# Two transformer layers with sliding-window attention: attention outputs laid out by head in DRAM, and loaded in two parts for the first and the last unit

## The chip, the core and the metric

The kernel runs on one core of a Trainium2 chip. The core has five engines that work side by side, each from a queue of its own that keeps its order: TensorE (PE in the profile; its weight loads are listed as PEld), VectorE (DVE), ScalarE (ACT), GpSimd (POOL) and SyncE (SP). SP computes nothing here; it issues transfers (DMAs). A transfer is moved by the core's 16 DMA engines. The metric is the device time of one execution, in microseconds.

## What is computed

Two layers, each an attention block and then a dense block with squared ReLU, both behind a layer normalisation and with a residual. The two layers share their weights. One sequence of S = 2048 rows, width D = 640, H = 32 heads of 20, a window of W = 256 rows, F = 1536:

```python
def _A_ref(x, wqkv, wo):
    qkv = (x @ wqkv).reshape(B, S, 3, H, Dh).transpose(2, 0, 3, 1, 4)
    q, k, v = qkv[0], qkv[1], qkv[2]
    scores = einsum("bhqd,bhkd->bhqk", q, k) * (Dh ** -0.5)
    mask = (i - j >= 0) & (i - j < W)
    p = softmax(where(mask, scores, -1e9))
    o = einsum("bhqk,bhkd->bhqd", p, v)
    return o.transpose(0, 2, 1, 3).reshape(B, S, D) @ wo

def _B_ref(x, w1, b1, w2, b2):
    r = maximum(x @ w1 + b1, 0)
    return (r * r) @ w2 + b2

for _ in range(2):
    x = x + _A_ref(_layernorm(x), A_wqkv, A_wo)
    x = x + _B_ref(_layernorm(x), B_w1, B_b1, B_w2, B_b2)
```

All is float32 in and out.

## The kernel before

**Units and quads.** The 2048 rows of a layer are cut into eight units of T = 256 rows; over both layers that makes 16 units, numbered u = 0 to 15. Each unit's attention is done in eight quads (NQ = 8) of four heads, which belong to two groups of GQ = 4 quads.

**Dense products** are made in fp16: each float32 operand is split into a rounded half and the rest (high and low), and three of the four products of halves are added up (line 327, the function `mm3`, for all of them, which is why the profile has one line for so much). Units pass through `stage_qk` and `stage_v` (q, k and v from wq_s), `stage_o` (output projection from wo_s), `stage_y` with a layer normalisation, and `stage_f` (w1_s, then w2_s with hh as the squared hidden values). Before the q, k and v products of a unit, its rows are normalised and transposed into yT: `ln_cross(u)` (line 455) for units from 3 on, `ln_t` for the first three.

**A quad of attention** has three steps. `max_quad` ("m") makes score products (lines 652 and 667) and DVE reduces them to row maxima with the mask (line 632). Each group's maxima are turned round by a transposing DMA (line 708) and written as rows into the operand qt (line 688). `exp_quad` ("s") makes the score products again with the maximum taken off (lines 756 and 764), ACT takes the exponentials into pt (line 778), and POOL masks them (lines 793 and 797). `pv_quad` ("v") multiplies by v, with a column of ones that gives the sums (line 827). Score products use two PSUM buffers, bb, so the next "m" can start only when ACT has read those of the "s" before it.

**Outputs.** ACT copies a quad's outputs (pv) into ot (line 839). Every second quad, SP writes both from ot to a DRAM tile o with four DMAs (line 844), one for each head of a quad, of 21 partitions: 20 values and the sum. `load_o` reads a unit's o back so that the products of `stage_o` can use it: the sums, each to four copies (rs, line 870), and the values (val, named od or ov, line 871). It also brings the unit's rows x for the residual (line 885). DVE then takes reciprocals (`ratio`, line 903) and multiplies (`times`, line 906), ACT rounds to the high half of od (line 910), DVE makes the low half (line 913); this goes by quarters of the columns. For most units `load_o(u - 1)` stands behind the first quad of unit u. For the first unit it stands behind its last quad; for the last unit behind everything, ahead of the last projection.

**Order.** The order on PE is worked out when the program is built: `together` interleaves a unit's quads with a stream of dense products, and `flow` does so for the first unit. For the four other engines a planner decides. `post` puts a job with an engine, a cost and a priority into a list that is sorted by priority, and `pump` issues the first job whose operands will be there by its own clock, or a later one that fits before it. `dma` posts to SP; `bulk` posts a weight load, issued by ACT; `need` and `wait_any` move the planner's time on. So a change of one job's cost, priority or operands can move many instructions, PE's too.

**Weights** are loaded once, in the first tens of microseconds, into space that is used for other things later, and split into halves by `convert` (ACT line 259, DVE line 260). `load_wo` loads wo in four pieces by d, and each of the five conversions waits for all four.

**SP's queue** holds, in the planner's order: the rows of maxima (708, 688), the writes of o (844), the loads of `load_o`, x rows, rows of b2 (951) and results (1049).

Of the kernel before, what the change touches and what calls it, by code (L numbers as in the profile page):

```python
# [10 lines left out]
F32 = mybir.dt.float32  # L11
F16 = mybir.dt.float16
# [9 lines left out]
H = 32  # L22
# [23 lines left out]
def kernel(ctx: ExitStack, tc: tile.TileContext, x, wqkv, wo, w1, b1, w2, b2, out):  # L46
# [408 lines left out]
    def ln_cross(u, *deps):  # L455

        ln_load(u, *deps)

        def dst():
            yTs[u] = sb.tile([P, 2, KC, T], F16, name="yT", tag="yT", bufs=1)  # L460
            return yTs[u]

        pre[u] = cross(lns.pop(u), dst, lambda: sb.tile([P, 2, 2, D], F16, name="yl", tag="qd", bufs=1))
# [349 lines left out]
    def pv_quad(n, quad):  # L813
# [18 lines left out]
        if qd == 0:  # L832
            ods[u] = tc.dram_tile([DH + 1, H, T], F32, name=f"o{u}")
        if qd % 2 == 0:
            ots[u] = sb.tile([P, 2, T], F32, name="ot", bufs=2)
        ot = ots[u]

        def out():
            nc.scalar.copy(ot[:, qd % 2], pv)  # L839

        def write():
            drv = ods[u].rearrange("d (q j) n -> j d q n", j=4)
            for j in range(4):
                nc.sync.dma_start(drv[j][:, qd - 1:qd + 1, :], ot[32 * j:32 * j + DH + 1])
# [10 lines left out]

    def load_o(u, late=False, free_=()):

        l, g = divmod(u, NG)
        if late:
            val = sb.tile([P, KC, T], F32, name="ov", tag="qt", bufs=2)  # L860
            od = sb.tile([P, KC, 2, T], F16, name="od", tag="yT", bufs=1)
        else:
            raw = sb.tile([P, 2, KC, T], F32, name="od", tag="hh", bufs=1)
            val = raw[:, 0]
            od = raw[:, 1].rearrange("p c n -> p (c n)").bitcast(F16).rearrange("p (c a n) -> p c a n", a=2, n=T)
        wrote = [ojobs.pop((u, qd)) for qd in range(1, NQ, 2)]
        rs = sb.tile([P, T], F32, name="rs", bufs=1)

        def load():
            nc.sync.dma_start(rs, ods[u][DH:].to_broadcast([4, H, T]))  # L870
# [28 lines left out]
        for i in range(4):  # L899
# [16 lines left out]
            j = post("D", 575, ratio, loaded, prio=pr)  # L916
# [175 lines left out]
    def together(ns, ms, dense, cost, share=1.0, whole=True, after=None, pace=0):  # L1092
# [23 lines left out]
        for k, (part_, what, m) in enumerate(ts):  # L1116
# [39 lines left out]
    def flow(todo, dense):  # L1156
# [3 lines left out]
        while todo:  # L1160
# [21 lines left out]
            else:  # L1182
                pv_quad(n, quad)
            pump()
# [97 lines left out]
```

## Time and profile before

| | |
|---|---|
| runs | 1594.38, 1593.18, 1589.94 us (median 1593.18) |
| the profiled execution | 1590.84 us, its span 1589.1 us |
| mean granted clock of TensorE | 0.997 |
| PE busy | 1558.1 us, 98% of the span |
| PEld | 1167.5 us, 73% |
| DVE, ACT, POOL busy | 983.8, 735.2, 599.5 us (62, 46, 38%) |
| moved by DMA | 160.44 MB, 243209 packets |

The span in 40 slices (one digit is the busy share in tenths, 9 is 90% or more; one slice is 39.7 us; PEclk is the clock that TensorE was granted):

```profile
PE   8989999999999999999999999999999999999999
DVE  8787665656756656665566656557665665756432
ACT  4555535444453444535343453544545345454522
PEclk9999999999999999999999999999999999999999
DMA  9763243362533525343362535434343352441020
```

A time that the chip measures for a whole execution is some 1.7 us more than the span between the first and the last instruction of its profile. Idle time of an engine other than PE costs nothing by itself. In the rows of a group, "3.3 [1.2 <-X]" means that the engine stood idle for 1.2 us just before and that X ended this; the number behind the start is the time to the end of the last instruction of the group.

### The profile page before, as it was taken

The numbers are of one execution on the slowest core, as the hardware profiler recorded it, in microseconds if no ns is written. First come the engines' busy times: TensorE is split into PE (matmuls) and PEld (weight loads), VectorE is DVE, ScalarE is ACT, GpSimd is POOL, SyncE is SP. The second block draws the span as 40 slices with busy tenths as digits, with TensorE's granted clock in tenths as the row PEclk, the third lists the DMA queues.
The fourth block names the chain that finished last, engine by engine and source line by source line (L and its number), as shares of the span: only waits on it lengthen the run. The fifth ranks groups of instructions, "written<-read, shape, count | busy, mean of one in ns | idle before, by whom it ended". The sixth has DMA issues, their size and how long they took to land.

```text
span 1589.1 us, 52465 instructions
## 1 busy us (share of the span) xinstructions
PE 1558.1 (98%) x21534; PEld 1167.5 (73%) x21534; DVE 983.8 (62%) x3253; ACT 735.2 (46%) x1593; POOL 599.5 (38%) x1291
## 2 busy tenths in 40 slices
PE   8989999999999999999999999999999999999999
PEld 7666767777777777778777777777777777776767
DVE  8787665656756656665566656557665665756432
ACT  4555535444453444535343453544545345454522
POOL 1234424334252443525323352442535235353512
PEclk9999999999999999999999999999999999999999
DMA  9763243362533525343362535434343352441020
GB/s 273 206 181 100 70 121 81 100 129 52 121 87 103 110 65 130 69 127 84 97 133 57 122 83 123 92 88 111 69 123 83 98 123 64 111 83 58 29 67 18
DMA packets 243209, 160.44 MB, mean 101 GB/s; under 512 B 91160, under 2 KB 226712, under 8 KB 242968
## 3 DMA queue, kind: packets, MB, share of 16 engines
q1 hardware_dynamic: 236600, 147.58, 38.8%
q10 hardware_dynamic: 6368, 9.50, 2.0%
q8 instruction: 169, 2.77, 0.7%
q14 instruction: 72, 0.59, 0.1%
HBM read 84.68 MB, written 52.95 MB: 87 GB/s over the span
## 4 chain that ended last, share of the span: by engine, by line
PE 91%; DVE 3%; ACT 2%; DMA 2%; SPq 1%; issue 1%; POOL 0%; ACTq 0%; DVEq 0%; POOLq 0%
PE acc L327 70%; PE pv L827 11%; PE bb L652 5%; PE bb L756 5%; DVE bb L632 1%; ACT pt L778 1%; DMA o<-ot 0%; PE bb L764 0%; DMA ov<-o 0%; PE bb L667 0%; SPq L688 0%; DVE qd L509 0%; DVE mx L632 0%; DMA qt<-qk 0%; DMA qk<-qd 0%
## 5 line engine op out<-in xcount | busy, mean ns | idle before, releaser
L778 ACT ACTIVATE pt<-bb 128x512 f32<-128x512 f32 (+1 forms) x736 | 376.9, 603 | 221.8 <-PE bb L756 198.9
L632 DVE CUSTOM_DVE_ANT_0 bb<-bb,maskq 128x320 f32<-128x320 f32 x896 | 409.2, 525 | 95.3 <-PE bb L652 88.6
L793 POOL TENSOR_SCALAR_AFFINE_SELECT pt<-pt 128x256 f32<-128x256 f32 x448 | 188.0, 422 | 558.1 <-ACT pt L778 545.3
L327 PE MATMUL acc<-y,w_s 128*128 128x256 f16 x2880 | 327.9, 273 | 2.1 <-ACT y L377 1.4
L327 PE MATMUL acc<-w_s,hh 128*128 128x320 f16 x2304 | 326.2, 299 | 0.0
L327 PEld LDWEIGHTS <-w_s 128*128 128x128 f16 x2880 | 276.6, 98 | 53.5 <-issue 17.7
L327 PEld LDWEIGHTS <-hh 128*128 128x128 f16 x2304 | 220.5, 98 | 98.4 <-issue 11.5
L327 PEld LDWEIGHTS <-wq_s 128*128 128x128 f16 x2400 | 230.0, 98 | 46.5 <-issue 13.8
L327 PE MATMUL acc<-yT,wq_s 128*128 128x256 f16 x2250 | 259.5, 273 | 2.1 <-DVE qd L509 0.7
L797 POOL TENSOR_SCALAR_AFFINE_SELECT pt<-pt 128x256 f32<-128x256 f32 x512 | 213.5, 438 | 89.2 <-ACT pt L778 87.6
L1012 DVE TENSOR_TENSOR hh<-r,hh 128x256 f16<-128x256 f32 x192 | 94.6, 513 | 213.2 <-ACT hh L1009 206.0
L827 PE MATMUL pv<-pt,vt 128*32 128x128 f32 (+1 forms) x3840 | 191.9, 330 | 0.7 <-POOL pt L797 0.6
L1006 POOL TENSOR_TENSOR r<-r 128x256 f32<-128x256 f32 x192 | 114.3, 615 | 169.5 <-ACT r L1002 167.2
L839 ACT COPY ot<-pv 128x256 f32<-128x256 f32 x128 | 47.8, 373 | 270.0 <-PE pv L827 266.1
L632 DVE DVE_READ_ACCUMULATOR2_ANT mx<- 128x1 f32 x1024 | 145.9, 143 | 0.0
L327 PE MATMUL acc<-wo_s,od 128*128 128x320 f16 x960 | 140.0, 301 | 3.8 <-ACT od L910 3.2
L827 PEld LDWEIGHTS pv<-pt,vt 128*32 128x32 f32 x3840 | 105.4, 109 | 42.1 <-POOL pt L797 6.9
L327 PE MATMUL acc<-wq_s,yT 128*128 128x320 f16 x900 | 131.8, 299 | 1.0 <-DVE y L378 0.5
L327 PEld LDWEIGHTS <-od 128*128 128x128 f16 x960 | 91.7, 98 | 48.7 <-issue 6.9
L1002 ACT ACTIVATE r<-acc,b1s 128x256 f32<-128x256 f32 x192 | 80.9, 473 | 95.9 <-PE acc L327 95.1
L327 PEld LDWEIGHTS <-yT 128*128 128x128 f16 x900 | 85.7, 98 | 39.2 <-issue 6.8
L364 POOL TENSOR_TENSOR bmv<-bmv,neghalf 128x1 f32<-128x1 f32 x64 | 44.2, 696 | 141.3 <-DVE bmv L358 140.8
(95 smaller groups left out, 1225.5 us busy)
## 6 DMA issues: line engine op xcount, KB each, us to landing
qt<-qk SPq DMA_DIRECT2D x30, 480.0 KB
kt<-qk SPq DMA_DIRECT2D x30, 480.0 KB
qk<-qd SPq DMA_DIRECT2D x17, 640.0 KB
o<-ot SPq DMA_DIRECT2D x256, 42.0 KB
od<-o SPq DMA_DIRECT2D x14, 640.0 KB
qk<-yl SPq DMA_DIRECT2D x13, 640.0 KB
qk<-qd SPq DMA_DIRECT2D x17, 320.0 KB
xt<-in_A_x_dram SPq DMA_DIRECT2D x16, 320.0 KB
```

Source lines behind the costliest of these rows:

```text
L327: nc.tensor.matmul(acc, lhs(a, c), rhs(b, c), start=(k == 0), stop=(k == 3 * nk - 1))
L632: nc.vector.tensor_tensor_reduce(out=v, in0=v, in1=mask, scale=1.0, scalar=-3.0e38, op0=ALU.add, op1=ALU.max, accum_out=accum[e, w]),
L652: nc.tensor.matmul(flat[e][rows, o:o + b - a], qt[r, p, i * P + 64 * h:i * P + 64 * (h + 1)], kt[r, p, a + to:b + to], start=True, stop=Tr ...
L756: nc.tensor.matmul(bb[e][rows, k, o + a:o + b], kt[r, 2 * qd + j, ko + 64 * h:ko + 64 * (h + 1)], qt[r, 2 * qd + j, q0 * P + a:q0 * P + b] ...
L778: nc.scalar.activation(box["pt"][:, :o], bb[e][:, k, :o], AF.Exp, scale=SCALE / (QS * QS))
L793: nc.gpsimd.affine_select(out=m, in_=m, pattern=[[0, 2], [-1, P]], compare_op=ALU.is_gt, fill=0.0, base=0, channel_multiplier=1)
L797: nc.gpsimd.affine_select(out=m, in_=m, pattern=[[0, 2], [1, P]], compare_op=ALU.is_ge, fill=0.0, base=0, channel_multiplier=-1)
L827: nc.tensor.matmul(pv[32 * jj:32 * (jj + 1), q0 * P:(q0 + qn) * P], vf[:, c:c + 32], pj[:, j, :], start=(k == 0), stop=(k == len(steps) - ...
L839: nc.scalar.copy(ot[:, qd % 2], pv)
L1002: nc.scalar.activation(box["r"], acc[:, f, :], AF.Relu, bias=b1s[:, f0 + f:f0 + f + 1], scale=1.0 / (YS * WS))
L1006: nc.gpsimd.tensor_tensor(box["r"], box["r"], box["r"], op=ALU.mult)
L1012: nc.vector.tensor_sub(hh[:, 1, f, :], box["r"], hh[:, 0, f, :])
```

## The change

There are six edits.

1. The DRAM tile o of a unit is [6, 32, 4, 256] in place of [21, 32, 256]: value 4c + d of a head lies at [c, head, d], and the sum at [5, head, 0], with three rows of padding behind it that are written but not read.
2. A quad is written when it is done, by four DMAs of 24 partitions (line 841 of the changed kernel). ot has room for one quad and four buffers, where it was two quads and two buffers. There are 512 such issues, of 24 KB each, in place of 256 of 42 KB.
3. Loaded rows of od are ordered (head, d) where they were (d, head), and those of wo_s accordingly: wo is loaded in five pieces by c, each a whole [128, 640] slice, and each conversion waits for its own piece alone.
4. A new function `begin_o` issues the loads of the sums and the values for the quads that are written. For the first and the last unit it is called behind the seventh quad, for seven of the eight quads (112 of 128 partitions); `load_o` then loads the last 16 partitions. For all other units `load_o` calls it once for all.
5. The division (`ratio`) waits for all parts; in the last unit the x rows wait for the last write of o.
6. `ln_cross(3)` posts its jobs with priority 1 in place of 2.

```diff
 def load_wo():
-    v = wo.rearrange("(h c d) n -> d h c n", c=KC, d=4)
+    v = wo.rearrange("(h c d) n -> c h d n", c=KC, d=4)
...
-    loads = []
-    for d in range(4):
-        loads.append(bulk(lambda d=d: nc.scalar.dma_start(raw[d * H:(d + 1) * H], v[d]), H * KC * D * 4, gate0))
     for c in range(KC):
-        woj[c] = convert(raw[:, c], wo_s[:, 0, c], wo_s[:, 1, c], D, loads[-1], *loads[:-1])
+        load = bulk(lambda c=c: nc.scalar.dma_start(raw[:, c], v[c]), P * D * 4, gate0)
+        woj[c] = convert(raw[:, c], wo_s[:, 0, c], wo_s[:, 1, c], D, load)
...
 def ln_cross(u, *deps):
-    ln_load(u, *deps)
+    prio = 1 if u == 3 else 2
+    ln_load(u, *deps, prio=prio)
...
-    pre[u] = cross(lns.pop(u), dst, lambda: sb.tile(...))
+    pre[u] = cross(lns.pop(u), dst, lambda: sb.tile(...), prio)
...
 def pv_quad(n, quad):
...
     if qd == 0:
-        ods[u] = tc.dram_tile([DH + 1, H, T], F32, name=f"o{u}")
-    if qd % 2 == 0:
-        ots[u] = sb.tile([P, 2, T], F32, name="ot", bufs=2)
-    ot = ots[u]
+        ods[u] = tc.dram_tile([KC + 1, H, 4, T], F32, name=f"o{u}")
+    ot = sb.tile([P, T], F32, name="ot", bufs=4)
     def out():
-        nc.scalar.copy(ot[:, qd % 2], pv)
+        nc.scalar.copy(ot, pv)
     def write():
-        drv = ods[u].rearrange("d (q j) n -> j d q n", j=4)
+        drv = ods[u].rearrange("c (q j) d n -> q j c d n", j=4)
         for j in range(4):
-            nc.sync.dma_start(drv[j][:, qd - 1:qd + 1, :], ot[32 * j:32 * j + DH + 1])
+            nc.sync.dma_start(drv[qd, j], ot[32 * j:32 * j + 4 * (KC + 1)])
     jobs.append(post("A", 262, out, prio=0))
-    if qd % 2:
-        ojobs[u, qd] = dma(write, 4 * (DH + 1) * 2 * T * 4, jobs[-1], n=4, cost=350.0)
+    ojobs[u, qd] = dma(write, 16 * (KC + 1) * T * 4, jobs[-1], n=4, cost=350.0)
...
+def begin_o(u, late, upto, *free_):
+    if u not in begun:
...
+        begun[u] = [val, od, sb.tile([P, T], F32, name="rs", bufs=1), 0, []]
+    val, od, rs, at, jobs = begun[u]
+    wrote = [ojobs.pop((u, qd)) for qd in range(at, upto)]
+    begun[u][3] = upto
+    def load():
+        nc.sync.dma_start(rs[16 * at:16 * upto], ods[u][KC, 4 * at:4 * upto, 0:1, :].to_broadcast([4 * (upto - at), 4, T]))
+        nc.sync.dma_start(val[16 * at:16 * upto], ods[u][:KC, 4 * at:4 * upto].rearrange("c h d n -> (h d) c n"))
+    jobs.append(dma(load, 16 * (upto - at) * (KC + 1) * T * 4, *wrote, *free_, n=2, prio=0))
+    return wrote
...
 def load_o(u, late=False, free_=()):
...
-    wrote = [ojobs.pop((u, qd)) for qd in range(1, NQ, 2)]
-    rs = sb.tile([P, T], F32, name="rs", bufs=1)
-    def load():
-        nc.sync.dma_start(rs, ods[u][DH:].to_broadcast([4, H, T]))
-        nc.sync.dma_start(val, ods[u][:DH].rearrange("(c d) h n -> (d h) c n", d=4))
-    loaded = dma(load, P * (KC + 1) * T * 4, *wrote, *free_, n=2, prio=0)
+    wrote = begin_o(u, late, NQ, *free_)
+    val, od, rs, _, parts = begun.pop(u)
+    loaded = parts[-1]
...
-            load_x(i, *([loaded] if u == 0 else ()))
+            load_x(i, *([loaded] if u == 0 else wrote if u == NU - 1 else ()))
...
-        j = post("D", 575, ratio, loaded, prio=pr)
+        j = post("D", 575, ratio, *parts, prio=pr)
...
 # together(), the quads of units 1 to 15, behind a pv_quad
+    if what[1] == NQ * NU - 2:
+        begin_o(NU - 1, True, NQ - 1)
...
 # flow(), the first unit, behind a pv_quad
+    if n == NQ - 2:
+        begin_o(0, False, NQ - 1)
```

What this makes of the instructions' order is shown at three places, on the engines that wait or are waited for there. A row is one instruction (or several alike, "x4") as it stands in an engine's queue, with its line; the changed kernel's lines differ a little from those before.

First, PE in the first quad of unit 2, where the score products of the exponentials (qt and kt_87, line 756, then 755) end and those of the next maximum (line 652) begin. Before:

```order
L756 LDWEIGHTS kt_87
L756 MATMUL bb_134<-qt,kt_87 64x192
L652 LDWEIGHTS qt
L652 MATMUL bb_133<-kt_86,qt 64x256
L652 LDWEIGHTS qt
L652 MATMUL bb_134<-kt_86,qt 64x256
```

After, at the same place:

```order
L755 LDWEIGHTS kt_87
L755 MATMUL bb_134<-qt,kt_87 64x192
L325 LDWEIGHTS wq_s
L325 MATMUL acc<-yT,wq_s 128x256
L325 LDWEIGHTS wq_s
L325 MATMUL acc<-yT,wq_s 128x256
```

Before, the maximum followed at once. Now q products of unit 3 follow, 30 of them, and then the maximum. One quad earlier, behind the exponentials of unit 1's eighth quad, products of the second dense layer stand, 28 before and 12 now, and the last of them run into the maximum:

```order
L325 LDWEIGHTS hh
L325 MATMUL acc<-w_s,hh 128x320
L325 LDWEIGHTS hh
L325 MATMUL acc<-w_s,hh 128x320
L651 LDWEIGHTS qt
L651 MATMUL bb_133<-kt_86,qt 64x256
```

Ahead of the exponentials of unit 1's seventh quad 68 of these products stand now, where 24 stood. In the first unit, PE's order is another too: the eight score products of one exponential step now stand between unit 2's transposes (10 small ones) and unit 2's first q products, and in two quads the "s" and the "m" behind it have only five (with a small transpose) and eight dense products between them.

Second, DVE round the first use of the attention outputs, behind the first reduction (line 632, then 631) of a maximum. rs are the sums, od the outputs; a row with w_s is the second half of a weight conversion. Before:

```order
L632 ISA bb_133,mx<-bb_133,maskq 128x320
L632 ISA mx 128x1
L903 RECIPROCAL rs<-rs 128x64
L906 TENSOR_TENSOR od<-od,rs 128x5x64
L903 RECIPROCAL rs<-rs 128x64 x2
L913 TENSOR_TENSOR od<-od 128x5x64
```

After:

```order
L631 ISA bb_133,mx<-bb_133,maskq 128x320
L631 ISA mx 128x1
L911 RECIPROCAL rs<-rs 128x64
L914 TENSOR_TENSOR od<-od,rs 128x5x64
L911 RECIPROCAL rs<-rs 128x64 x2
L260 SCALAR_TENSOR_TENSOR w_s<-vt_93,w_s 128x640
L921 TENSOR_TENSOR od<-od 128x5x64
```

The reduction stands ahead of the division in both. A conversion of a weight slice has come between the reciprocals and the low half of od. On ACT its first half stands between the copy of the last quad's outputs and the rounding of od:

```order
L836 COPY ot<-pv 128x256
L259 ACTIVATE w_s<-vt_93 128x640
L918 CAST od<-od 128x5x64 x3
```

Before, the rounding followed the copy at once. Third, SP at the end of the program, from the last rows of maxima on. Before:

```order
L688 DMA qt<-mt 1x8x128 x4
L844 DMA o_26024<-ot 21x2x256 x8
L885 DMA x_27223<-xs_127 128x640
L885 DMA x_27223<-xs_128 128x640
L870 DMA rs<-o_26024 128x1x256
L871 DMA ov<-o_26024 128x5x256
```

After:

```order
L687 DMA qt<-mt 1x8x128 x4
L841 DMA o_26327<-ot 6x4x256 x8
L870 DMA rs<-o_26327 112x1x256
L871 DMA ov<-o_26327 112x5x256
L841 DMA o_26327<-ot 6x4x256 x4
L870 DMA rs<-o_26327 16x1x256
L871 DMA ov<-o_26327 16x5x256
L893 DMA x_27548<-xs_127 128x640
L893 DMA x_27548<-xs_128 128x640
```

Seven eighths are loaded ahead of the last write, one eighth behind it, and the x rows have moved behind the loads.

More of the change, by code (lines that the diff above doesn't have):

```diff
@@ L854 @@
     ols = {}
+    begun = {}
+    def begin_o(u, late, upto, *free_):
+        if u not in begun:
+            if late:
+                val = sb.tile([P, KC, T], F32, name="ov", tag="qt", bufs=2)
+                od = sb.tile([P, KC, 2, T], F16, name="od", tag="yT", bufs=1)
+            else:
+                raw = sb.tile([P, 2, KC, T], F32, name="od", tag="hh", bufs=1)
+                val = raw[:, 0]
+                od = raw[:, 1].rearrange("p c n -> p (c n)").bitcast(F16).rearrange("p (c a n) -> p c a n", a=2, n=T)
+            begun[u] = [val, od, sb.tile([P, T], F32, name="rs", bufs=1), 0, []]
[7 more added lines that the diff above has]
+        return wrote
     def load_o(u, late=False, free_=()):
         l, g = divmod(u, NG)
[L859 to L865, printed above, removed]
-        wrote = [ojobs.pop((u, qd)) for qd in range(1, NQ, 2)]
-        rs = sb.tile([P, T], F32, name="rs", bufs=1)
-        def load():
-            nc.sync.dma_start(rs, ods[u][DH:].to_broadcast([4, H, T]))
-            nc.sync.dma_start(val, ods[u][:DH].rearrange("(c d) h n -> (d h) c n", d=4))
-        loaded = dma(load, P * (KC + 1) * T * 4, *wrote, *free_, n=2, prio=0)
+        wrote = begin_o(u, late, NQ, *free_)
+        val, od, rs, _, parts = begun.pop(u)
+        loaded = parts[-1]
         if u == NU - 1:
```

2 lines of the change are left out of this document (1 added, 1 removed).

## The prediction

> **What bounds the kernel now.** I read the busy times by stretches first, then TensorE's waits, then the timeline round each wait. Two of the four stretches of 96.58 us, one unit of 256 rows each, that I looked at (columns: stretch, length, busy time of PE, PEld, DVE, ACT, POOL, granted clock, DMA share, GB/s):
>
> ```profile
> 300.00:396.58 96.58, 96.58 (x1412) 72.81 (x1410) 60.21 (x200) 45.36 (x98) 38.25 (x84) 1.00 0.41 97
> 589.74:686.32 96.58, 96.58 (x1412) 72.81 (x1410) 60.15 (x200) 45.36 (x98) 38.25 (x84) 1.00 0.42 97
> ```
>
> PE is busy for the whole of a unit in the middle, at full clock, and DVE has over a third of its time free. There the new layout can gain nothing; it can only lose, by making PE wait. Something can be gained where PE waits: in the first 210 us and from 1370 us on. The two dearest kinds, in us, times, longest:
>
> ```profile
> PE bb L652 <- ACT pt L778: 8.9, 8, 2.7
> PE acc L327 <- ACT od L910: 3.2, 2, 2.3
> ```
>
> The longest of them, the half clock behind it (window rows), and a shorter one late in the program, behind which the clock stays:
>
> ```profile
> 201.47 0.75 PE L756 MATMUL bb<-qt,kt 62*64 62x192 f16 x32
> 202.31 3.05 ACT L778 ACTIVATE pt<-bb 128x512 f32<-128x512 f32 x6 [3.13 <-PE bb L756]
> 204.93 0.27 PE L652 MATMUL bb<-kt,qt 60*64 60x256 f16 x1 [2.70 <-ACT pt L778]
> 205.42 0.75 PE L652 MATMUL bb<-kt,qt 60*64 60x256 f16 x37 [0.23 <-ACT pt L778]
> 203.34:206.75 3.41, 1.60 (x54) 1.14 (x57) 0.43 (x2) 2.03 (x5) 2.66 (x8) 1.00 0.73 224
> 206.76:210.16 3.40, 3.40 (x34) 2.03 (x27) 3.36 (x16) 0.37 (x1) 0.00 (x0) 0.50 0.94 293
> ...
> 1376.75 0.75 PE L756 MATMUL bb<-qt,kt 62*64 62x192 f16 x32
> 1377.44 1.67 PE L327 MATMUL acc<-wo_s,od 128*128 128x320 f16 x11
> 1380.21 0.27 PE L652 MATMUL bb<-kt,qt 60*64 60x256 f16 x1 [1.10 <-ACT pt L778]
> 1376.70:1380.10 3.40, 2.41 (x44) 1.63 (x44) 1.55 (x5) 2.50 (x6) 1.67 (x5) 1.00 1.14 216
> ```
>
> In both places the score products of the next maximum (L652) start 3.46 us after those of the exponentials (L756): ScalarE must first empty the banks. Dense products standing between fill that time; at 202 us none stand there. A half clock follows a window with 1.60 us of work in 3.41, none follows one with 2.41 in 3.40.
>
> **Unit 3's normalisation.** Ranked higher, it lets the q products of unit 3 be ready when unit 2's first quad has started its exponentials: 30 of them stand there now. The attention's place moves with it: 68 products of the second dense layer run ahead of unit 1's seventh quad, and only 12 behind its eighth. At 1.67 us for 11, 12 take 1.8; with 0.7 for L756, 0.95 of the 3.46 us stay idle where 2.70 were: 1.75 won. The clock: 3.4 us at 0.50 cost half of it, 1.7, and 0.95 idle is less than the 1.10 behind which it stayed at 1380 us. I take -3.4. Bounds: 0, if the 68 products only postpone the wait; -4.6 (2.70 + 0.23 + 1.7), if nothing of it is left.
>
> The Trainium skill, page "TensorE: Matmul & The Clock Gate", part 1, says that the array falls to half rate after at least one idle window of some 3.4 us. By that rule these waits cost no clock, and the term would be -1.75. Here the trace differs: clock 0.50 stands behind waits of 2.70 and 0.23 us.
>
> **Seven of eight quads ahead, at the end.** The last unit's outputs are written, read back, divided by their sums and split before the output projection (the line with 6.25 is of the chain of waits, the last of the page's DMA issues):
>
> ```profile
> 1517.21 1.34 SPq L844 DMA_DIRECT2D o<-ot  x4
> 1519.92 0.59 SPq L870 DMA_DIRECT2D rs<-o  x1
> 1520.56 6.25 DMA ov<-o
> 1525.84 0.96 DVE L903 RECIPROCAL rs<-rs 128x64 f32<-128x64 f32 x2 [1.92 <-DMA rs<-o]
> 1529.16 0.45 PE L327 MATMUL acc<-wo_s,od 128*128 128x320 f16 x2 [0.88 <-ACT od L910]
> 1529.87 1.40 PE L327 MATMUL acc<-wo_s,od 128*128 128x320 f16 x9 [0.27 <-DVE od L913]
> ...
> ov<-o SPq DMA_DIRECT2D x2, 640.0 KB
> ```
>
> 640 KB take 6.25 us, and PE waits 0.88 + 0.27. Now seven eighths go out behind the seventh quad, on SP ahead of the eighth's write, whose data is not there before 1517.2 anyway. The last eighth, 80 KB, need only land 1.2 us sooner than 6.25 for both waits to go; at half of 6.25, taken as an upper estimate for an eighth of the bytes, it is 3 us sooner: -1.15. PE's order there is the same as before. The x rows that now follow the loads on SP are first needed behind the projection's products. Bounds: 0 and -1.15.
>
> **The start.** PE's order is another here, and three things count. First, the wait for unit 2's transposed input:
>
> ```profile
> 69.64 0.70 PE L327 MATMUL acc<-wq_s,kt 128*128 128x320 f16 x4 [1.00 <-DVE yT L378]
> 66.80:70.20 3.40, 1.98 (x11) 1.07 (x11) 3.14 (x13) 1.23 (x3) 0.00 (x0) 1.00 0.73 234
> 70.23:73.63 3.40, 3.40 (x20) 1.94 (x20) 1.71 (x4) 1.64 (x4) 1.53 (x4) 0.50 1.01 310
> 77.90 0.50 PE L764 MATMUL bb<-qt,kt 62*128 62x256 f16 x8
> 78.34 1.67 PE L327 MATMUL acc<-wq_s,kt 128*128 128x320 f16 x11
> 79.94 0.73 PE L667 MATMUL bb<-kt,qt 60*128 60x128 f16 x8
> ```
>
> A quad's 8 exponential products (0.5 to 0.8 us) now stand between the transposes and that wait: -0.8. The window then holds some 2.6 us of work, more than the 2.41 that kept the clock: -1.7. Second, two quads get shorter cover: L667 came 2.04 us after L764 with 11 products between and no wait; five products and a small transpose (0.8) behind 0.5 leave some 0.6 open, eight (1.1) some 0.4: together +1.0.
>
> Third, the first use of the outputs (with a conversion of a weight slice on ACT and on DVE, L259 and L260):
>
> ```profile
> 112.85 0.75 PE L652 MATMUL bb<-kt,qt 60*64 60x256 f16 x37 [0.23 <-ACT pt L778]
> 113.74 0.50 DVE L632 CUSTOM_DVE_ANT_0 bb<-bb,maskq 128x320 f32<-128x320 f32 x1 [0.73 <-issue]
> 114.16 0.55 DVE L903 RECIPROCAL rs<-rs 128x64 f32<-128x64 f32 x1
> 115.48 0.37 ACT L839 COPY ot<-pv 128x256 f32<-128x256 f32 x1 [2.69 <-PE pv L827]
> 117.69 0.45 PE L327 MATMUL acc<-wo_s,od 128*128 128x320 f16 x2 [2.29 <-ACT od L910]
> 118.02:121.42 3.40, 3.13 (x13) 1.74 (x13) 3.40 (x13) 0.48 (x2) 0.00 (x0) 0.50 1.22 205
> 103.59 0.73 ACT L259 ACTIVATE w_s<-kt 128x640 f16<-128x640 f32 x1
> 109.21 0.82 DVE L260 SCALAR_TENSOR_TENSOR w_s<-vt,w_s 128x640 f16<-128x640 f32 x1
> ```
>
> PE waits 2.29 us here, and loading ahead does not remove it. The division is queued on DVE behind the first reduction (L632) of a maximum that PE starts at 112.85, and it stands there still. What is new is a weight slice between: ACT converts it (0.73) after the copy of pv and before the first cast of od, DVE (0.82) behind that and before it splits od. Both lie on the chain from 112.85 to 117.69, partly beside each other: +1.0, nearer to the longer one with what waits on both than to their sum. Its bounds: -4.3 (2.29 + 0.27 at 118.4 us and the clock's 1.7) and +1.6. The start together: -0.8 - 1.7 + 1.0 + 1.0 = -0.5.
>
> **More writes, and the wo loads.** 256 issues of o become 512, and SP's four take 1.34 us. In the middle they are hidden in SP's spare time, at a price of nothing; what it costs without that cover is the first rival. wo comes in five loads of whole slices in place of four that all had to land; its conversions start earlier on ACT and DVE, which is in the new orders that I counted above.
>
> **Sum.** -3.4 - 1.15 - 0.5 = -5.05. The profiled execution took 1590.84 us (span 1589.1 and 1.7 round it), so 1585.8. It lies 2.3 below the median of the three runs, 1593.18, from which the same sum gives 1588.1. I forecast **1586.5**, nearer to the run whose rows I used; its own range is 1582 to 1588.4.
>
> **Rivals.** (1) Slower: SP becomes the brake. Behind a write of o that waits for ScalarE's copy stand the transposed maxima (L708) and the rows of qt (L688), and the next exponentials' products wait for these:
>
> ```profile
> 633.07 3.64 SPq L688 DMA_DIRECT2D qt<-mt  x4
> 641.33 0.75 PE L756 MATMUL bb<-qt,kt 62*64 62x192 f16 x32
> ...
> 1369.91 3.62 SPq L688 DMA_DIRECT2D qt<-mt  x4
> ```
>
> From the rows' last issue (636.71) to their use pass 4.62 us; 3.22 were enough at 1373.53 to 1376.75. That leaves 1.40 us in the tightest group of a unit. One more write (1.34) just fits. It decides from the second on: 2 x 1.34 - 1.40 = 1.3 us per unit, 13 units, +17: 1590.8 - 4.55 + 17 = 1603. For it: SP keeps order, and each transpose now has a write ahead. Against it: a write's data is copied well before the maxima behind it are reduced. Chance 0.13. The skill's page "DMA: Bandwidth & Descriptors", Rules for kernel authors, warns against transfers under 64 KB as mostly overhead; these shrink from 42 to 24 KB, and no row here shows PE paying for it.
>
> (2) The change does less than it says: the clock drops remain or come elsewhere, as by the skill's rule they have nothing to do with such waits. Then -5.05 + 3.4 = -1.7: 1589.1 from the profiled run, 1591.5 from the median. For it: the window of 66.8 us had 1.98 us of work and still lost its clock, so the threshold is not sharp. Chance 0.19.
>
> (3) The start's wait goes as well: -4.3 in place of +1.0, sum -10.4, 1580.5. For it: seven eighths are loaded early. Against it: the reduction ahead of the division. Chance 0.10.
>
> **Numbers.** The forecast's case has 0.58. A measurement of this kernel tells 0.3% (4.8 us) from no change, that is below 1588.4. Faster: 0.58 + 0.10 = 0.68; within: 0.19; slower: 0.13. Range: from 1580, the third rival, to 1594, the second with the median's offset and some loss in the middle; left out are the first rival and the far ends.
>
> **What would show it.** Right, if PE's wait for pt near 200 us is about 1 us and no clock of 0.50 follows; if no wait for od stands before the last projection; if one for od, with clock 0.50 behind it, still stands before the first, some 3 us long; if a middle unit still takes 96.58 us with PE busy throughout. Wrong, if PE waits for L688's rows in the middle, if the half clock near 70 us stays, or if a new wait follows the 68 products.

## The result and the profile after

| | before | after |
|---|---|---|
| median of the runs | 1591.95 us (6 runs, 1589.94 to 1594.38) | 1601.71 us (6 runs, 1596.09 to 1605.65) |
| profiled execution, span | 1590.84, 1589.1 us | 1605.03, 1603.3 us |
| PE busy | 1558.1 us | 1567.1 us |
| mean granted clock | 0.997 | 0.994 |

The change made the kernel slower: the ratio is 1.0057, with a 95% interval of 1.004 to 1.0074, and the medians lie 9.8 us apart. 1586.5 was forecast, and 1594 was the end of the range. The profiled execution is one of the longest of its six, so sizes below come from medians and places from the trace.

PE's waits after the change (us in total, times, longest):

```profile
PE bb L651 <- ACT pt L777: 7.7, 8, 2.6
PE acc L325 <- ACT od L918: 3.3, 1, 3.3
PE pv L826 <- POOL pt L796: 2.8, 7, 0.9
PE bb L666 <- ACT pt L777: 2.7, 1, 2.7
```

The first two rows look as before. New are a wait of `pv` for POOL's masks and one of 2.7 us of a maximum (L666) in the first unit. The middle of the program shows most. This is the stretch from the first `pv` product of unit 3 to that of unit 14, where PE's order is the same in both, before and then after (length, busy time of PE, PEld, DVE, ACT, POOL, clock, DMA share, GB/s):

```profile
309.76:1362.26 1052.50, 1052.47 (x14950) 792.26 (x14946) 653.11 (x2177) 488.44 (x1062) 409.73 (x892) 1.00 0.42 98
```

```profile
317.63:1374.44 1056.81, 1055.04 (x14949) 792.69 (x14945) 652.53 (x2177) 485.34 (x1062) 411.30 (x892) 1.00 0.42 98
```

The same work takes 4.3 us more. 1.7 of them are idle time, and by 2.6 the products' busy time is longer, at full clock. PE comes to unit 3 later by 7.9 us (317.63 less 309.76), though that stretch holds the place where 3.4 were to be won.

Three places went as forecast. Unit 2's first quad, where the wait was 2.70 us with a half clock behind it, and the window behind the wait:

```profile
205.79 1.80 PE L325 MATMUL acc<-w_s,hh 128*128 128x320 f16 x12
208.55 0.27 PE L651 MATMUL bb<-kt,qt 60*64 60x256 f16 x1 [0.96 <-ACT pt L777]
```

```profile
208.01:211.42 3.41, 2.64 (x73) 1.75 (x73) 1.58 (x8) 1.08 (x4) 1.78 (x5) 1.00 0.27 103
```

The last projection follows the products ahead of it with no wait for od. (The last unit is still no shorter in this execution, 142.56 us behind 1460.74 where it was 140.91 behind 1448.19: two half clocks of 3.41 us fall into it, at up to 1.7 us each, and none before.)

```profile
1530.82 11.58 PE L325 MATMUL acc<-w_s,hh 128*128 128x320 f16 x84
1542.32 8.58 PE L325 MATMUL acc<-wo_s,od 128*128 128x320 f16 x60
```

And a wait for od of 3.3 us still stands before the first projection, as the list of waits shows.

**The middle.** Each write of o takes SP longer. The durations of SP's issues (least, median, most in ns), before and after:

```profile
L844 SPq DMA_DIRECT2D o<-ot x256: 267/311/1677, 58.3 to 1518.2; - x128
```

```profile
L841 SPq DMA_DIRECT2D o<-ot x512: 670/687/1806, 49.1 to 1533.6; - x171
```

There are twice as many, and each takes 0.69 us in place of 0.31, though it carries 24 KB and no longer 42. Four of them now hold SP for 2.9 us, eight times a unit. What this does is seen in unit 5 (timeline; after, SP, then POOL, ACT and PE, here and below one engine behind another; ... stands for rows of the same engine that are left out):

```profile
550.49 2.95 SPq L841 DMA_DIRECT2D o<-ot  x4
...
554.81 1.52 SPq L959 DMA_DIRECT2D xt<-in_B_b_dram  x1
562.98 3.31 POOL L966 TENSOR_TENSOR x<-x,xt 128x320 f32<-128x320 f32 x4 [1.79 <-DMA xt<-in_B_b_dram]
...
568.50 0.41 POOL L792 TENSOR_SCALAR_AFFINE_SELECT pt<-pt 128x256 f32<-128x256 f32 x1 [1.07 <-ACT pt L777]
566.90 0.41 ACT L1017 CAST hh<-r 128x256 f16<-128x256 f32 x1 [2.90 <-POOL r L1014]
...
567.78 0.59 ACT L777 ACTIVATE pt<-bb 128x512 f32<-128x512 f32 x1
573.76 1.18 PE L826 MATMUL pv<-pt,vt 128*32 128x256 f32 x8 [0.28 <-POOL pt L796]
```

The same place before:

```profile
540.81 1.38 SPq L844 DMA_DIRECT2D o<-ot  x4
...
543.19 1.45 SPq L951 DMA_DIRECT2D xt<-in_B_b_dram  x1
551.89 3.31 POOL L958 TENSOR_TENSOR x<-x,xt 128x320 f32<-128x320 f32 x4
555.81 0.41 ACT L1009 CAST hh<-r 128x256 f16<-128x256 f32 x1 [1.08 <-POOL r L1006]
...
557.35 0.60 ACT L778 ACTIVATE pt<-bb 128x512 f32<-128x512 f32 x1 [0.56 <-PE bb L756]
```

Unit 5 starts 9.27 us later after the change (its first `pv` product at 512.19 for 502.92). Take that off, and the b2 rows (line 959) are issued 2.35 us later than before and POOL's addition of them starts 1.82 us later. POOL squares the hidden values behind it; ACT, which keeps order, stands at the rounding of these squares (2.90 us) and starts the exponentials 1.16 us late; POOL's masks are late, and PE's `pv` products wait for them. Four engines hand on a delay that began at SP.

### The profile page after: what moved, and what is told of

It reads as the page before. It is cut to its first block, busy times and chain, and to the rows that moved or that the text cites. A ratio compares the mean times of both kernels' runs of the same rounds, so it can differ in the third digit from the quotient of the medians.

```text
span 1603.3 us, 52930 instructions
## 1 busy us (share of the span) xinstructions
PE 1567.1 (98%) x21534; PEld 1170.5 (73%) x21534; DVE 983.7 (61%) x3253; ACT 731.2 (46%) x1593; POOL 600.1 (37%) x1291
## 4 chain that ended last, share of the span: by engine, by line
PE 82%; DMA 4%; DVE 4%; ACT 4%; POOL 3%; SPq 2%; issue 1%; ACTq 0%; POOLq 0%; DVEq 0%
PE acc L325 62%; PE pv L826 10%; PE bb L755 4%; PE bb L651 4%; ACT pt L777 2%; DMA xt<-in_B_b_dram 2%; DVE bb L631 2%; SPq L841 1%; POOL r L1014 1%; POOL x L966 1%; DMA qk<-qd 1%; ACT r L1010 1%; POOL pt L796 1%; SPq L687 1%; DMA o<-ot 0%
## 5 line engine op out<-in xcount | busy, mean ns | idle before, releaser
L826 PE MATMUL pv<-pt,vt 128*32 128x128 f32 (+1 forms) x3840 | 195.8, 332 | 3.4 <-POOL pt L796 2.8
```

Source lines behind the costliest of these rows:

```text
L826: nc.tensor.matmul(pv[32 * jj:32 * (jj + 1), q0 * P:(q0 + qn) * P], vf[:, c:c + 32], pj[:, j, :], start=(k == 0), stop=(k == len(steps) - ...
```

## The experiments

All ran against the kernel before, whose median in these comparisons was 1591.9 to 1592.3 us. The 95% interval of a ratio to it reaches 1.4 to 2.4 us either way (2.7 for the changed kernel), so a step of 2 us from one run to another is not certain by the medians alone. The line numbers of a run are its own.

**1. The writes' shape: plain blocks (run four_plain).**

```diff
-        ods[u] = tc.dram_tile([KC + 1, H, 4, T], F32, name=f"o{u}")
+        ods[u] = tc.dram_tile([H, P // 4, T], F32, name=f"o{u}")
...
-            nc.sync.dma_start(drv[qd, j], ot[32 * j:32 * j + 4 * (KC + 1)])
+            nc.sync.dma_start(ods[u][4 * qd + j, :4 * (KC + 1)], ot[32 * j:32 * j + 4 * (KC + 1)])
...
-    v = wo.rearrange("(h c d) n -> c h d n", c=KC, d=4)
+    v = wo.rearrange("(h d c) n -> c h d n", c=KC, d=4)
```

The loads follow this order of rows; it holds for all later runs but b2_by_act and those made from the kernel before.

> The changed kernel, but a head's 24 rows lie together in DRAM, so that each of the 512 writes is one plain block of 24 rows of 256 and no longer 6 x 4 x 256; same number of writes, same bytes, same order on TensorE. Theory A (the shape makes an issue on SP 0.69 us long, and the b2 rows behind the writes come late): an issue takes about 0.3 us, POOL no longer waits for the b2 rows, a middle unit takes 96.58 us again, and the 6.5 us that were lost between unit 2 and unit 14 are gone: about 1595. Theory B (it is the number of writes, whatever their shape): waits and time as in the changed kernel, about 1602.

1595.75 us, ratio 1.0024 (1.0015 to 1.0033): 6.0 under the changed kernel. SP's issues and the middle stretch:

```profile
L840 SPq DMA_DIRECT2D o<-ot x512: 289/363/2217, 51.4 to 1524.9; - x171
```

```profile
316.01:1368.48 1052.47, 1052.45 (x14949) 792.21 (x14945) 653.00 (x2177) 487.63 (x1062) 409.49 (x892) 1.00 0.44 99
```

With as many writes of as many bytes, an issue takes 0.36 us, and the middle is as long as before the change. Theory A holds: it is the form of the transfer that makes SP slow. The 6.5 us that the expectation names were its 4.3 and some 2 in unit 2.

**2. One write for each quad (run one_write).**

```diff
-            for j in range(4):
-                nc.sync.dma_start(...)
+            nc.sync.dma_start(ods[u][4 * qd:4 * qd + 4].rearrange("h d n -> (h d) n"), ot)
```

> As the run before, but with one write of 128 rows of 256 for each quad (32 rows a head, 8 of them never read): 128 issues in place of 512, 128 KB each. Theory A: SP is as free as before the change or freer, a middle unit takes 96.58 us, about 1595. Theory B: the same 1595, since the number is small, so that it parts from A only in the run before. Theory C (the new order of work on the engines is what costs in the middle, not SP): waits as in the changed kernel, about 1602. If the bytes moved count (a third more per write), it is slower than the run before.

1594.14 us, ratio 1.0014 (1.0005 to 1.0023). A quarter of the issues brings 1.6 us more, which the two intervals do not tell from nothing. The Trainium skill, page "DMA: Bandwidth & Descriptors", Rules for kernel authors, advises to join transfers under 64 KB. In these runs joining four times 24 KB into 128 KB brought 1.6 us, and the form of the 24 KB is worth 6.0.

**3. The b2 rows off SP's queue (run b2_by_act).** The changed kernel with its dear writes, and one edit:

```diff
-        load = dma(lambda: nc.sync.dma_start(b2s, ...), P * D * 4)
+        load = dma(lambda: nc.scalar.dma_start(b2s, ...), P * D * 4)
```

> The changed kernel with its dear writes; only the b2 rows are issued from ScalarE's queue and no longer from SP's, behind the writes. Theory A1 (the b2 rows' lateness is the link from SP to PE): POOL waits for xt vanish from the middle, the drift between unit 3 and unit 13 (3.7 us in the profile of the changed kernel, 4.3 from unit 3 to unit 13) goes, about 1596 to 1597, a little less gained than with plain writes, since an issue takes ScalarE's time. Rival A2 (it is the rows of maxima or the loads of o behind the writes): waits stay, about 1602.

1595.31 us, ratio 1.0017 (1.0005 to 1.0028): 6.4 under the changed kernel, a little more than expected. POOL's waits for the b2 rows (us, times, longest), before and after the change and in this run, and this run's middle:

```profile
POOL x L958 <- DMA xt<-in_B_b_dram: 9.3, 2, 7.6
```

```profile
POOL x L966 <- DMA xt<-in_B_b_dram: 26.4, 13, 7.7
```

```profile
POOL x L966 <- DMA xt<-in_B_b_dram: 8.0, 1, 8.0
```

```profile
312.13:1365.07 1052.94, 1052.70 (x14949) 792.42 (x14946) 651.00 (x2177) 487.54 (x1062) 412.10 (x892) 1.00 0.42 98
```

SP still spends 0.69 us on each of 512 issues, and the loss is gone. So the link from SP to PE in the middle is this one load, not the rows of the maxima. (PE waited for these rows for 1.1 us in all after the change, 0.90 of them in unit 2; with plain writes, in four_plain, 0.62 us stand there.)

**4. Unit 3's ranking alone (run prio_only).** The kernel before, with `prio = 1 if u == 3 else 2` in `ln_cross`.

> The kernel before with one edit: unit 3's normalisation at priority 1. The prediction's term: the wait of 2.70 us near 202 us becomes about 0.95, and the half clock behind it goes: -3.4, about 1588.5. Rival 1 (the clock's drop has nothing to do with the wait): -1.75, about 1590. Rival 2 (the wait only moves): 1592.

1589.09 us, ratio 0.9983 (0.9974 to 0.9992): -3.1, where -3.4 was forecast. The wait is 0.42 us here, with 16 products in front and no half clock behind. The profiled executions bear it out in place: from a wait of 0.52 us in unit 1 (141.61 us before, 142.11 here) to one of 1.10 us in unit 14 (1380.21 and 1377.15) this run takes 3.56 us less. That is more than the 2.28 us that the wait itself lost.

**5. The slice loads in the kernel before (run wo_slices).**

```diff
-        v = wo.rearrange("(h c d) n -> d h c n", c=KC, d=4)
+        v = wo.rearrange("(h c d) n -> c d h n", c=KC, d=4)
...
+            load = bulk(lambda c=c: nc.scalar.dma_start(raw[:, c], v[c]), P * D * 4, gate0)
+            woj[c] = convert(raw[:, c], wo_s[:, 0, c], wo_s[:, 1, c], D, load)
```

> The kernel before with one edit: wo in five loads by slice, each conversion waiting for its own. This alone gives the start of TensorE's order in the changed kernel (to unit 1's second quad). Theory S (the start is lost by this order: short cover, a weight slice in the chain of the first od): some 8 us lost by unit 1's fifth quad, as in the profile of the changed kernel, about 1600, with a wait of 2.7 us for pt near 60 us and one of about 3 us for od near 120 us. Rival (the start is lost by the dear writes on SP): within 1 us of before, about 1592.

1602.25 us, ratio 1.0065 (1.005 to 1.008). The size is near the 1600 expected, but its place is not:

```profile
50.26 0.37 PE L762 MATMUL bb<-qt,kt 62*128 62x256 f16 x1 [5.39 <-DVE bmv L356]
```

This wait of 5.39 us and one of 3.24 (at 53.87, for the rows of maxima) stand at the very start, before any od; the changed kernel has none of this size there. DVE, on which the first depends, stood for 5.52 us until rows of x had landed. Rows of o in the kernel before are ordered (d, head), so a slice had to be a [4 x 32 x 640] load here and was [32 x 4 x 640] in the change. This run therefore says nothing of the change's start. The Trainium skill, page "DMA: Bandwidth & Descriptors", section "Why a DMA increments its semaphore by 16 and not by 1", says that a load runs on the largest number of engines, up to 16, that divides the slowest dimension of both its sides, which here would be 4. That would fit, and no run separates it.

**6. wo in four loads again (run wo_four).** The one-write run with

```diff
-            woj[c] = convert(..., load)
+            woj[c] = convert(..., loads[-1], *loads[:-1])
```

and four loads of 32 partitions.

> The run with one write for each quad, but with wo loaded in four pieces again, each conversion waiting for all four, as in the kernel before. Theory S (the start is lost by the new way of loading wo): the one-write run lost 6 us against before until unit 2's first quad, apart from unit 3's ranking; without it 1588 to 1589, below the kernel before by 3 to 4 and at or below the run with the ranking alone. Rival (the start's loss comes from writing quad by quad): about 1594, as the one-write run. The order near the first od has no dense products between the exponentials and the next maximum, so a wait of about 3 us may stand there in place of the one for od.

1593.31 us, ratio 1.0001 (0.9987 to 1.0014): the expectation was missed by some 5 us, and the rival's 1594 is nearer. The profiled execution took 1588.12, but the twelve runs lie between 1587.93 and 1599.05. The wait for od is gone, and waits of 2.43, 2.01 and 2.38 us round it took its place.

**7. Slices and quads, one at a time (runs slices_alone, quads_alone).** Both with plain writes, the ranking, and no early load. slices_alone keeps the slice loads and writes after every second quad; quads_alone writes after each and loads wo in four pieces.

```diff
 # slices_alone
-        ojobs[u, qd] = dma(write, 16 * (KC + 1) * T * 4, jobs[-1], n=4, cost=350.0)
+        if qd % 2:
+            ojobs[u, qd] = dma(write, 4 * (DH + 1) * 2 * T * 4, jobs[-1], n=4, cost=350.0)
 # quads_alone
-            woj[c] = convert(..., load)
+            woj[c] = convert(..., loads[-1], *loads[:-1])
```

> Of the changed kernel the slice loads of wo and unit 3's ranking, with plain writes after every second quad and no early load; rows by head, so that a slice is one [32 x 4 x 640] load as in the changed kernel and not [4 x 32 x 640] as in the run with slices before. With writes by quad too it is the no-early-load run (1593.1), without both it is the run with the ranking alone (1589.1). Theory S (the slices' order costs): about 1593. Theory Q (writing quad by quad makes the worse order): about 1589.

> The other half: one plain write after each quad and unit 3's ranking, wo in four loads, no early load. Theory S: about 1589. Theory Q: about 1593. If both are near 1591, the loss is shared.

1592.26 us (1.0002; 0.9993 to 1.001) and 1595.60 us (1.0022; 1.0011 to 1.0033). With the next run they make a square: neither 1589.1, slices 1592.3, quads 1595.6, both 1593.05. Each costs against the ranking alone, and together they don't cost the sum. Theory S and theory Q are both too simple: each edit changes the planner's order of the first 200 us into another one with its own waits.

**8. The early loads (runs no_early_load, early_at_end).** The one-write run with both calls of `begin_o` ahead of time left out, and with the first unit's left out.

```diff
 # both runs
-                if n == NQ - 2:
-                    begin_o(0, False, NQ - 1)
 # no_early_load alone
-                if what[1] == NQ * NU - 2:
-                    begin_o(NU - 1, True, NQ - 1)
```

> The one-write run without the early load: both the first and the last unit load all eight quads at once; TensorE's order is the same. The prediction's term for the end: waits of 0.9 + 0.3 us for od before the last projection come back, +1.15, and at the start nothing changes, because the reduction and the weight slice stand ahead of the division: about 1595.3. Rival (the early load shortens the start's chain too): the wait for od near 119 us grows beyond 3.9 us, 1596 or more.

> The one-write run (1594.1, early load for the first and the last unit) with the early load for the last unit alone; TensorE's order is the same. Theory E (the end's term pays about 1.5, the first unit's early load costs 2 to 3, because the planner then puts a weight slice and a maximum's reduction ahead of the division): the wait for od near 117 us is 2.3 + 0.3 us as in the no-early-load run and not 3.9, no wait for od stands before the last projection, about 1591.5. Rival (the early load does nothing measurable at either end): 1593 to 1594.

1593.05 us (1.0003; 0.9994 to 1.0012) and 1591.45 us (0.9996; 0.9985 to 1.0006), against 1594.14 with both. For the first, 1595.3 was expected: the first unit's early load does count, and against the kernel. The second came out at 1591.5 as theory E says, with 2.29 us of wait before the first projection. At the end the early load takes out waits of 1.48 + 0.28 us, and the median falls by 1.6. In the first unit it costs 2.7. The profiled executions bear out both in place. Up to the wait of 0.52 us in unit 1, one_write takes 147.22 us and early_at_end 143.60. And from the wait of 1.86 us for pt in the last unit to that of 1.40 us before its dense block, executions with no half clock between take 89.05 us (before) and 89.09 (prio_only) without the early load, 87.51 (four_plain) and 87.71 (one_write) with it. Round the first projection, with both early loads (one_write):

```profile
118.77 0.37 ACT L836 COPY ot<-pv 128x256 f32<-128x256 f32 x1 [3.70 <-PE pv L826]
119.03 0.74 ACT L259 ACTIVATE w_s<-vt 128x640 f16<-128x640 f32 x1
119.70 0.46 ACT L916 CAST od<-od 128x320 f16<-128x320 f32 x1
122.56 3.84 PE L325 MATMUL acc<-wo_s,od 128*128 128x320 f16 x13 [3.90 <-ACT od L916]
```

without them (no_early_load):

```profile
114.30 0.66 DVE L912 TENSOR_TENSOR od<-od,rs 128x320 f32<-128x320 f32 x1
117.30 0.37 ACT L836 COPY ot<-pv 128x256 f32<-128x256 f32 x1 [3.61 <-PE pv L826]
117.57 0.46 ACT L916 CAST od<-od 128x320 f16<-128x320 f32 x1
119.51 0.45 PE L325 MATMUL acc<-wo_s,od 128*128 128x320 f16 x2 [2.30 <-ACT od L916]
```

With the early load the planner puts a weight slice (L259) between the copy and the rounding, and on DVE a reduction ahead of the division; without it there is neither. In no_early_load the rounding starts 2.6 us after the first quarter of od is divided (114.96), and the copy of `pv`, ahead of it on ACT, waits for PE in this time. In one_write the division itself ends only at 119.66 (it runs for 0.49 us from 119.17, behind 1.65 us for which the profile names no releaser), so there the copy is not all that holds the rounding up.

**9. The rounding ahead of the copy (run cast_first).**

```diff
-        jobs.append(post("A", 262, out, prio=0))
+        jobs.append(post("A", 262, out, prio=2 if n == NQ else 0))
```

> The no-early-load run (1593.1) with one instruction moved: on ScalarE the first rounding of od stands ahead of the copy of pv of unit 1's first quad and no longer behind it; every other engine's order is the same. Theory P (the prediction's: the division, behind the reduction on DVE, holds the first od up): no change of the wait of 2.3 us before the first projection, 1593. Theory K (ScalarE's copy, which waits for pv, holds it up, since the division is done 2.6 us before the rounding in the no-early-load run): the wait falls to about 1 us, since the second rounding still stands behind the copy; 1591 to 1592, less if a half clock goes with it.

1594.35 us, ratio 1.0013 (1.0004 to 1.0022), where theory K expected 1591 to 1592, so nothing was won. But:

```profile
115.89 0.46 ACT L916 CAST od<-od 128x320 f16<-128x320 f32 x1 [2.12 <-DVE od L912]
117.50 0.37 ACT L836 COPY ot<-pv 128x256 f32<-128x256 f32 x1 [1.15 <-PE pv L826]
118.28 4.50 PE L325 MATMUL acc<-wo_s,od 128*128 128x320 f16 x30 [0.89 <-ACT od L916]
126.19 2.54 PE L325 MATMUL acc<-wo_s,od 128*128 128x320 f16 x12 [3.40 <-DVE x L944]
```

The wait for od falls from 2.30 to 0.89 as theory K says, and 3.40 us appear a few products later: DVE stands for 3.01 us until the residual's rows x have landed, the projection's results can't be taken off, and PE waits for DVE. In this execution the next load in SP's queue set the end of that stretch. Such a wait, of 2.29 us, stands in four_plain's execution too, which has not this edit; so the run shows what held od up, and not what the edit is worth.

**10. What paid, together (run end_only).** Ranking, plain writes after every second quad (singly for the last two quads of the last unit), four loads of wo, early load at the end.

```diff
 # against the kernel before
+        prio = 1 if u == 3 else 2
...
+            for q in qs:
+                nc.sync.dma_start(ods[u][4 * q:4 * q + 4].rearrange("h d n -> (h d) n"), ot[:, q % 2])
...
+                if what[1] == NQ * NU - 2:
+                    begin_o(NU - 1, True, NQ - 1)
```

> What is left when only the parts that paid are kept: unit 3's ranking, plain writes of 128 rows (two after every second quad, as the planner had it before), wo in four loads, the early load for the last unit alone. TensorE's order is exactly that of the run with the ranking alone (1589.1). Theory (the end's term of the prediction holds): its waits of 0.98 + 0.27 us for od before the last projection go, about 1588, 4 us under the kernel before. Rival (as in the first unit, an early load costs more than it brings): 1589 or more.

1589.91 us, ratio 0.9991 (0.9982 to 1.0). 1588 was expected, and the median falls on the rival's side (1589 or more); it doesn't part from the ranking alone (0.9974 to 0.9992). No od wait stands before its last projection, so the 1.2 us are gone there, but the total doesn't show them. Both versions are well below the changed kernel; the ranking alone is the one that is clear of no change.

## Why the prediction was wrong

Medians, each run one part away from the next:

| part | from, to (us) | measured | forecast |
|---|---|---|---|
| unit 3's ranking | 1592.2, 1589.1 | -3.1 | -3.4 |
| slices and writes by quad: a new order, above all at the start | 1589.1, 1593.05 | +4.0 | -0.5 for both rows of the start |
| early load at the end | 1593.05, 1591.45 | -1.6 | -1.15 |
| the start: early load for the first unit | 1591.45, 1594.14 | +2.7 | (in the -0.5) |
| four writes for a quad, not one | 1594.14, 1595.75 | +1.6 | 0 |
| each of them 6 x 4 x 256 | 1595.75, 1601.71 | +6.0 | 0 |

The rows add up to +9.5, and -5.05 was forecast. Of the 14.5 us between them the two rows of the writes make some 7.6, and the new order and the first early load, where the start was to win 0.5, some 7. A row under 2 us is not certain by itself; for the end the traces bear it out (1.4 in place, run 8), for four writes against one they don't. The +4.0 need not all lie in the start: the profiled executions of the two runs part by 1.0 us up to the wait of 0.52 us in unit 1. Later, a longer wait for od at the end (1.48 for 0.98 us) and a half clock more stand in the second.

**Unit 3: right**, in place and size. 0.95 us of wait were forecast and 0.96 stand there; the 68 products left no wait behind. The clock stays at 1.00. By the rule that the prediction cites from the Trainium skill, page "TensorE: Matmul & The Clock Gate", part 1, the term would have been -1.75. The interval of the run with the ranking alone, -1.3 to -4.1 us, holds both; the half clock that went from this place and the 3.56 us that its trace won round it speak for -3.4.

**The end: right.** Both waits went, PE's order was the same, and the stretch is 1.4 us shorter where no half clock falls into it. That this pays in the total is seen in one pair of medians (-1.6) and not in the other (end_only against the ranking alone, +0.8).

**More writes: the step that failed.** "SP's four take 1.34 us" was carried over from a 21 x 2 x 256 write to one of 6 x 4 x 256. The new one takes 2.9. With 1.34 the sentence "in the middle they are hidden" would have held: with plain writes (1.45 for four) the middle is 1052.47 us long. The trace before had a warning in SP's own list: its rows of maxima, 1 x 8 x 128, take 0.63 us an issue with only 2 KB.

**The first rival** had the engine and the mechanism, and not the place: its slack of 1.40 us was that of the rows of maxima, whereas the b2 rows broke first, and its 17 us for 13 units were some 6. It let one more write of 1.34 us just fit; what broke the fit was the length of an issue.

**The start: wrong, sign and all.** Waits were taken from the trace before and moved to a new order one by one. Taken one by one in the changed kernel's trace, they came out as follows.

The 0.8 us ahead of unit 2's first products were not won. Waits of 0.56, 0.24 and 1.00 us stood round its transposes before; 0.61, 0.73 and 0.52 us stand there now.

The half clock near 70 us came earlier in this execution, from 64.64 us on, behind a wait that the forecast had put at nothing. There 20 products stand between the exponentials and the next maximum, as before. But ACT, which keeps order, stood at a rounding of q (line 505) until a transfer out of the same buffer had landed, with three of the four exponentials behind it:

```profile
61.92 0.60 ACT L505 ACTIVATE qd<-acc 128x512 f16<-128x512 f32 x1 [2.91 <-DMA qk<-qd]
63.34 0.76 PE L666 MATMUL bb<-kt,qt 60*128 60x128 f16 x8 [2.72 <-ACT pt L777]
```

Seven more runs have this order of PE there (1, 2, 3, slices_alone, both of 8, and 9). In their profiled executions this wait is 1.0 to 1.4 us, and only four_plain has a half clock between 60 and 76 us. So the term for the clock held in six of eight executions, and the wait in its place was left out.

The short cover of two quads (together +1.0) cost less. The maximum waited for ACT behind neither; ahead of the five products PE waited 0.77 us for DVE's low half of q, where 0.6 had been put. (By the prediction's own figures, 2.04 - 0.8 - 0.5, it would have been 0.74.)

The wait for od grew by 1.0 (3.32 against 2.29), as forecast, and the two conversions that were named stand in it. Wrong was the premise that the division, behind the reduction, holds the first od up:

```profile
119.00 0.49 DVE L914 TENSOR_TENSOR od<-od,rs 128x320 f32<-128x320 f32 x1
120.08 0.37 ACT L836 COPY ot<-pv 128x256 f32<-128x256 f32 x1 [3.57 <-PE pv L826]
120.35 0.74 ACT L259 ACTIVATE w_s<-vt 128x640 f16<-128x640 f32 x1
120.98 0.45 ACT L918 CAST od<-od 128x320 f16<-128x320 f32 x1
121.12 0.82 DVE L260 SCALAR_TENSOR_TENSOR w_s<-vt,w_s 128x640 f16<-128x640 f32 x1 [0.75 <-ACT w_s L259]
```

The first quarter was divided at 119.49 us, and ACT's copy of `pv` came only at 120.08. Before, too, the rounding followed the copy (115.48 and 0.37 us). Run 9 shows the same for an order with no reduction ahead.

One half clock was counted behind this wait, as before. The trace has three: from 115.85 to 119.26 and from 122.68 to 129.50 us. Two more cost up to 3.4 us; the other runs with this order of PE have two to four.

So the step that failed at the start is to carry waits over singly, with ACT's other work and further half clocks at nothing. Why slices and quads cost 3.2 and 6.5 alone and 4.0 together stays open: the orders differ at many places, and each has its own waits.

The third rival did not come: the first od wait did not go. Of the second a part did. The clock behind unit 3's wait held, but half clocks came elsewhere: the profiled execution has six windows of them, the one before three.

## What to carry to other kernels

Before counting a changed transfer at an old price, find a row with its own shape: here the same 24 KB cost SP 0.36 or 0.69 us an issue, and that alone made 6 us. When a queue becomes slower, look for the load in it with the least slack, over all that share the queue and not only over the ones that PE names, and follow it through the engines that keep order. A gain that is sized in one place (unit 3) could be kept without the rest of the change; the start, whose order comes from a planner, was not priced rightly by moving its waits one by one.

## What the runs showed of the hardware

- The length of an issue on SP went by form and not by size here (medians): 128 x 256 in one block 0.34 us, 24 x 256 in one block 0.36, 21 x 2 x 256 0.31, 6 x 4 x 256 0.69. In the last the 24 partitions are cut in two dimensions; that this is the cause was not tried.
- The same pair of waits costs a half clock in one execution and none in another. Before, waits of 1.86 and 0.58 us begin at 1454.40; after, 1.85 and 0.58 at 1466.95. Before, the pair falls into two windows, with 1.77 us of PE's work in the first and 2.61 in the second, and the clock stays at 1.00. The first:

```profile
1452.63:1456.04 3.41, 1.77 (x40) 1.16 (x33) 3.33 (x8) 2.74 (x6) 1.56 (x4) 1.00 0.05 10
```

After, it falls into one, with a half clock behind it:

```profile
1467.50:1470.92 3.42, 1.55 (x54) 1.09 (x57) 3.42 (x9) 2.86 (x7) 3.08 (x6) 1.00 0.02 2
1470.93:1474.34 3.41, 3.41 (x35) 1.79 (x24) 3.21 (x16) 0.39 (x2) 0.15 (x1) 0.50 0.04 8
```

The windows are counted from the clock's changes: after, those at 64.64 and 1470.93 us lie 412 steps of 3.4133 us apart; before, those at 70.23 and 206.76 us lie 40 apart. The Trainium skill, page "TensorE: Matmul & The Clock Gate", part 1, says that the window is 3413 ns and free-running; the trace agrees. The page has the half clock come after at least one idle window; here it came behind windows with 1.55, 1.60 and 1.98 us of work. Nor does the work in a window decide it alone: 1.77 us kept the clock and 1.98 lost it. Each half-clock window costs up to 1.7 us, and two to seven stand in the profiled executions, which is part of why the times of one kernel scatter by some us.
